# Attention with a position bias and a gated MLP on one core: k and q of the last-row tile change queue, and k gets a second buffer

## The chip, the cores and the metric

The kernel runs on one core of one Trainium2 chip. The metric is the device time of one execution in microseconds (us). The kernel before takes 732.81 us, the median of 3 runs (729.6 to 733.76). One more execution was profiled; it took 731.07 us, with a span of 729.3 us between its first and last instruction. An effect under about 0.5% of the time can't be told from none by such measurements.

## The reference

There are 4 batches, 8 heads, 576 positions and 64 values per head. Each head adds a learned bias, the output of a small network of the distance between two positions, to its scores; after the softmax the result goes through a gated MLP with 512 inputs and 1536 hidden values.

```
scores = scale * np.matmul(q, k.transpose(0, 1, 3, 2))
x = (psi_rel / psi_i)[..., None]
h = np.maximum(x @ w1 + b1, 0.0)
scores = scores + (h @ w2).transpose(2, 0, 1)[None, :, :, :]
attn = softmax(scores)
y = np.matmul(attn, v)                    # back to 2304 x 512
out = ((y @ w_a) * (y @ w_b)) @ w_out
```

## The kernel before

The attention is cut into units. A unit is a batch, a pair of heads and one of two chunks of query rows. The first chunk holds rows 0 to 255, the second rows 256 to 575, so there are 32 units, and the last 16 are of the second chunk. A unit of the first chunk has four tiles of 128 query rows (two per head); a unit of the second chunk has five: A2, B2, A3, B3 and T. T is the mixed last-row tile: it holds the 64 rows that are left (512 to 575) of both heads, 64 partitions for each.

A tile passes through these steps. PE makes the scores into PSUM (`qk`, L533, or L514 for T). DVE adds the bias and takes the row extremum (L561), ACT takes the exponential and the row sum (L566), POOL adds a small number to the sum (L611), DVE takes its reciprocal (L612), POOL scales the row into half precision (`ph`, L596), and DVE makes the low part of it (L599). SP then issues a transposing DMA (L605) that turns `ph` into `pt`. When all tiles of a unit are turned, PE multiplies them with v (`pv`, L657), and ACT and DVE write the result as the input of the MLP (`x`, L670 and L672). The MLP's products (`ab`, L791, and `o`, L835) stand between the attention's products on PE, in an order that the program writes out (`merge`). The attention ends at about 612 us; from there the MLP of the last rows runs alone.

The order on PE is fixed by the program throughout, and that on DVE from the second half of the program. The order on ACT, POOL and SP is chosen by a planner that simulates the program with its own costs: an instruction goes to its engine's list when its inputs and a buffer for its output are there in the simulation, the earlier one of the program first. On the chip every engine and every queue then works through its list in that order, so an instruction that waits holds up all that stand behind it.

SP's queue carries nearly all transfers of this part: the bias rows (`bias`, L498 and L501), k and q of the ordinary tiles (`rk`, `rq`, L423 and L424), v (`rv`, L236), k and q of T (`kt`, L468, two DMAs of 64 partitions, and `qt`, L470), and the transposes (L605). The queue of ACT carries the outputs and, earlier, stores of the bias (L205). The queue of POOL carries DMAs only at the start of the kernel: 16 stores of the bias (also L205).

`load_kt` is called once per unit of the second chunk, at the unit's first tile. `kt` and `qt` live in the pool `xp`, which is opened when the memory of the bias stage (pool `bg2`) comes free. `kt` has one buffer, so the load for the next unit can only start when T's products of this unit have read it; `qt` has two.

Of the kernel before, what the change touches and what calls it, by code (L numbers as in the profile page):

```python
# [9 lines left out]
F32 = mybir.dt.float32  # L10
# [13 lines left out]
HB = S // 2  # L24
# [6 lines left out]
TOK = 256  # L31
# [23 lines left out]
def attention_moe(ctx, tc, q0d, q1d, kd, vd, idn, wp, wa, wb, wo, lsw, lg, rl, out):  # L55
    nc = tc.nc
# [9 lines left out]
    xt, cpool, epool, xpool, ypool = [], [None], [None], [None], [None]  # L66
# [395 lines left out]

    def load_kt(u):
        b, hp, _ = UNITS[u]
        kt = xpool[0].tile([128, 2, HB], F32, tag="kt", name="kt", bufs=1)
        for hf in range(2):
            src = kd[b, hp, :, hf * HB:hf * HB + HB].rearrange("(j d) n -> d j n", j=2)
            nc.sync.dma_start(out=kt[64 * hf:64 * hf + 64], in_=src)  # L468
        qt = xpool[0].tile([128, 2, TAIL], F32, tag="qt", name="qt", bufs=2)
        nc.sync.dma_start(out=qt, in_=q1d[b, hp, :, :, TOK:])  # L470
        st["kt", u], st["qt", u] = kt, qt

    def prep_v(u):
# [209 lines left out]
    def attn_steps():  # L683
        vgen = [None]
        for n in range(NT + 4):
# [16 lines left out]
            for ahead, un in ((a, TILES[n + a][0]) for a in (6, 4, 3, 1, 0, -1) if 0 <= n + a < NT and FIRST[TILES[n + a][0]] == n + a):  # L702
                if un < NP:
                    continue
                if ahead == 6:
                    load_unit(un)
                elif ahead == 4:
                    b, hp, c = UNITS[un]
                    st["raw", un] = *st["raw", un][:2], load_v(b, hp, whole=un < NF)
                elif ahead == 3:  # L710
                    lows[0] = n >= SOON
                    with late():
                        prep_k(un)
                        prep_q(un)
                elif ahead == int(not NF <= un < B * NP):
                    lows[0] = n >= SOON
                    with late():
                        prep_v(un)
                if ahead == 0 and UNITS[un][2]:
                    load_kt(un)  # L720
# [341 lines left out]
```

## Time and profile before

| what | us |
|---|---|
| three runs | 733.76, 729.6, 732.81 |
| profiled execution | 731.07 |
| its span | 729.3 |
| PE busy in the span | 693.7 (95%) |
| DVE busy | 463.0 (63%) |
| ACT busy | 437.4 (60%) |
| POOL busy | 284.0 (39%) |

The profile is that of one execution. Busy time is the time in which an engine had an instruction in work; DMA issues are not counted as busy, except that those of POOL stand in its line. A share over the whole span mixes stages with different limits, and the stage that the change touches, from about 305 to 600 us, has to be read by itself.

### The profile page before, as it was taken

The page shows a single profiled execution, that of the slowest core. Times are in us where ns is not written, and L with a number is a line of the kernel's source. Part 1 is how long each engine was busy: PE and PEld are TensorE (multiplying, and loading weights), DVE is VectorE, ACT ScalarE, POOL GpSimd, SP SyncE. Part 2 cuts the span into 40 slices and gives each one's busy share as a digit, 9 for nine tenths or more (in the row PEclk, how much of TensorE's full clock was granted, in tenths as well). Part 3 has the DMA queues.
Part 4 walks back from the last instruction along what each step waited for, and adds up shares of the span by engine and source line. Part 5 has one row for each costly group of instructions (what it writes and reads, how often), then busy time and mean ns, then how long its engine had stood idle before and what let it go on. Part 6 is the DMA issues. An engine that isn't in the chain of part 4 may idle for free.

```text
span 729.3 us, 15665 instructions
## 1 busy us (share of the span) xinstructions
PE 693.7 (95%) x5535; PEld 534.0 (73%) x5535; DVE 463.0 (63%) x1150; ACT 437.4 (60%) x957; POOL 284.0 (39%) x435
## 2 busy tenths in 40 slices
PE   7889899999999999999899999989999999999997
PEld 1255477778886665777688788878888888888886
DVE  6666388876645676667898889878987871201100
ACT  5887588879967777744566566546655643312310
POOL 3444233336751132333454355435643663311200
PEclk9999999999999999999899999999999999999999
DMA  8989678788745997898999999999999985000001
GB/s 244 329 306 339 231 243 269 225 272 282 257 140 136 213 207 168 205 225 207 243 250 253 252 244 247 252 256 253 245 271 240 224 146 134 1 15 15 2 14 44
DMA packets 178163, 147.69 MB, mean 203 GB/s; under 512 B 125092, under 2 KB 138148, under 8 KB 178084
## 3 DMA queue, kind: packets, MB, share of 16 engines
q1 hardware_dynamic: 170928, 130.91, 71.4%
q10 hardware_dynamic: 5876, 10.93, 5.3%
q0 software_dynamic: 1280, 4.84, 1.8%
q8 instruction: 44, 0.72, 0.4%
q14 instruction: 35, 0.29, 0.1%
HBM read 101.14 MB, written 17.18 MB: 162 GB/s over the span
## 4 chain that ended last, share of the span: by engine, by line
PE 60%; DMA 9%; issue 9%; ACT 7%; DVE 7%; POOL 7%; SPq 1%; POOLq 0%; DVEq 0%; ACTq 0%
PE ab L791 25%; PE o L835 14%; PE pv L657 6%; DMA pt<-ph 5%; PE qk L533 4%; PE psta L184 3%; POOL ph L596 3%; PE tp L629 3%; POOL sm L611 2%; ACT p L566 1%; PE pr L912 1%; DVE ks L438 1%; DVE p L561 1%; POOL gl L811 1%; DVE ph L599 1%
## 5 line engine op out<-in xcount | busy, mean ns | idle before, releaser
L791 PEld LDWEIGHTS <-w16t 128*128 128x128 f16 x2592 | 247.3, 98 | 43.3 <-issue 11.9
L791 PE MATMUL ab<-x,w16t 128*128 128x256 f16 x2304 | 270.2, 273 | 1.0 <-DVE x L672 1.0
L566 ACT ACTIVATE p<-p,mn 128x576 f32<-128x576 f32 x144 | 111.6, 775 | 80.7 <-DVE mn L561 64.2
L599 DVE SCALAR_TENSOR_TENSOR ph<-p,sm,ph 128x64 f16<-128x64 f32 x192 | 106.6, 595 | 29.4 <-POOL ph L596 29.2
L561 DVE CUSTOM_DVE_ANT_0 p<-qk,bias 128x576 f32<-128x576 f32 x143 | 106.6, 747 | 28.4 <-PE qk L533 12.0
L835 PE MATMUL o<-wos,gh 128*128 128x512 f32 x384 | 120.6, 395 | 0.0
L596 POOL TENSOR_SCALAR ph<-p,sm 128x576 f16<-128x576 f32 x96 | 71.8, 748 | 106.7 <-DVE sm L612 96.4
L611 POOL TENSOR_SCALAR sm<-sm 128x1 f32<-128x1 f32 x144 | 54.4, 378 | 146.9 <-ACT p L566 144.6
L811 POOL TENSOR_TENSOR gl<-g,gh 128x256 fp32r<-128x256 f32 x96 | 72.9, 760 | 94.4 <-ACT gh L810 94.1
L775 DVE SCALAR_TENSOR_TENSOR g<-ab,wv,asb 128x256 f32<-128x256 f32 x84 | 40.3, 480 | 77.6 <-ACT asb L799 77.0
L810 ACT CAST gh<-g 128x256 fp32r<-128x256 f32 x96 | 38.8, 404 | 72.8 <-DVE g L775 72.8
L835 PEld LDWEIGHTS o<-wos,gh 128*128 128x128 f32 x384 | 69.5, 188 | 16.9 <-issue 4.5
L835 PE MATMUL o<-wos,gl 128*128 128x512 f32 x192 | 75.0, 391 | 0.0
L533 PE MATMUL qk<-ks,qs 128*128 128x288 f32 x384 | 72.8, 311 | 2.1 <-DVE mn L561 1.2
L533 PEld LDWEIGHTS qk<-ks,qs 128*128 128x128 f32 x384 | 56.1, 189 | 10.9 <-issue 5.3
L617 POOL TENSOR_SCALAR p<-p,sm 128x576 f32<-128x576 f32 x48 | 47.0, 979 | 22.6 <-DVE sm L612 16.1
L799 ACT ACTIVATE asb<-ab,wv 128x256 f32<-128x256 f32 x84 | 39.4, 469 | 25.4 <-PE ab L791 24.8
L657 PE MATMUL pv<-pt,vs 128*64 128x320 f16 (+1 forms) x560 | 42.2, 304 | 7.1 <-DMA pt<-ph 7.1
L657 PEld LDWEIGHTS <-vs 128*64 128x64 f16 x560 | 32.0, 112 | 19.0 <-issue 10.7
L612 DVE RECIPROCAL sm<-sm 128x1 f32<-128x1 f32 x144 | 22.7, 157 | 30.5 <-POOL sm L611 28.7
L835 PEld LDWEIGHTS o<-wos,gl 128*128 128x128 f32 x192 | 36.0, 188 | 7.8
L438 DVE TENSOR_TENSOR ks<-rk,ks 64x576 fp32r<-64x576 f32 x48 | 39.6, 825 | 3.2 <-ACT ks L441 1.8
(105 smaller groups left out, 855.3 us busy)
## 6 DMA issues: line engine op xcount, KB each, us to landing
bias<-bias_d SPq DMA_DIRECT2D x127, 288.0 KB, 4.1
rv<-vd SPq DMA_DIRECT2D x32, 320.0 KB, 4.5
rk<-kd SPq DMA_DIRECT2D x24, 288.0 KB, 3.5
wraw<-wa SPq DMA_DIRECT2D x12, 511.8 KB, 6.2
wraw<-wb SPq DMA_DIRECT2D x12, 511.8 KB, 6.5
wraw<-wo SPq DMA_DIRECT2D x12, 511.8 KB, 5.1
bias_d<-bo ACTq DMA_DIRECT2D x20, 295.5 KB, 3.8
bias_d<-bo POOLq DMA_DIRECT2D x16, 295.5 KB, 6.7
```

The lines of the kernel that those rows point to most:

```text
L438: nc.vector.tensor_tensor(out=ks[ol, j], in0=rk[sl], in1=ks[sl, j].bitcast(F32), op=ALU.subtract)
L533: nc.tensor.matmul(ps[:, hf, :HB], a, b[:, hf * HB:hf * HB + HB], start=(x == 0), stop=(x == len(prods) - 1))
L561: ttr = nc.vector.tensor_tensor_reduce(out=p.rearrange("p (a n) -> p a n", a=2), in0=ps[:, :, :HB], in1=bt.rearrange("p (a n) -> p a n", a=2),
L566: exps.append(nc.scalar.activation(p, p, AF.Exp, bias=mn, scale=-1.0, accum_out=sm))
L596: nc.gpsimd.tensor_scalar(out=ph[:, :S], in0=p, scalar1=rc, scalar2=1.0, op0=ALU.mult, op1=ALU.mult)
L599: ins = nc.vector.scalar_tensor_tensor(out=ph[:, o:o + c1 - c0], in0=p[:, c0:c1], scalar=rc, in1=ph[:, c0:c1], op0=ALU.mult, op1=ALU.subtract,
L611: nc.gpsimd.tensor_scalar(out=sm, in0=sm, scalar1=1e-9, scalar2=1.0 / (PS if u >= NF else 1.0), op0=ALU.add, op1=ALU.mult)
L617: nc.gpsimd.tensor_scalar(out=p, in0=p, scalar1=rc, scalar2=1.0, op0=ALU.mult, op1=ALU.mult)
L657: nc.tensor.matmul(ps[64 * j:64 * j + 64, o:o + N], v[:, j, :], p[:, j * N:j * N + N], start=(x == 0), stop=(x == len(prods) - 1),)
L791: nc.tensor.matmul(ab[:, j], w16[nm, f][:, pw, kk, :], xs[px][:, kk, :], start=(x % (3 * KC) == 0), stop=(x % (3 * KC) == 3 * KC - 1),)
L811: nc.gpsimd.tensor_tensor(out=gl, in0=g, in1=gh.bitcast(F32), op=ALU.subtract)
L835: nc.tensor.matmul(o, g[:, sl], wos[f][:, p], start=(f == 0 and x == 0), stop=(f == FC - 1 and x == 2))
```

## The change

`kt` has two buffers in place of one, and the three DMAs of `load_kt` are issued on POOL's queue in place of SP's. What is loaded, and from where, is the same.

```diff
     def load_kt(u):
         b, hp, _ = UNITS[u]
-        kt = xpool[0].tile([128, 2, HB], F32, tag="kt", name="kt", bufs=1)
+        kt = xpool[0].tile([128, 2, HB], F32, tag="kt", name="kt", bufs=2)
         for hf in range(2):
             src = kd[b, hp, :, hf * HB:hf * HB + HB].rearrange("(j d) n -> d j n", j=2)
-            nc.sync.dma_start(out=kt[64 * hf:64 * hf + 64], in_=src)
+            nc.gpsimd.dma_start(out=kt[64 * hf:64 * hf + 64], in_=src)
         qt = xpool[0].tile([128, 2, TAIL], F32, tag="qt", name="qt", bufs=2)
-        nc.sync.dma_start(out=qt, in_=q1d[b, hp, :, :, TOK:])
+        nc.gpsimd.dma_start(out=qt, in_=q1d[b, hp, :, :, TOK:])
         st["kt", u], st["qt", u] = kt, qt
```

## Rows read from the trace of the kernel before

**Rows 1.** Engines' busy us (instructions), clock, DMA share, GB/s in three stretches.
```profile
330.00:600.00 270.00, 262.22 (x2215) 217.64 (x2208) 225.84 (x535) 157.36 (x362) 130.15 (x203) 0.99 1.11 241
...
350.00:354.00 4.00, 3.87 (x28) 2.90 (x27) 3.91 (x8) 0.63 (x3) 1.13 (x2) 0.50 1.10 293
354.00:358.00 4.00, 4.00 (x32) 3.32 (x31) 3.71 (x10) 3.25 (x8) 2.21 (x4) 0.82 1.07 265
```

**Rows 2.** Waits of PE, 364 to 600 us: total us, times, longest.
```profile
PE pv L657 <- DMA pt<-ph: 3.5, 4, 2.0
```

**Rows 3.** Groups by line and shape, 330 to 600 us: busy us, mean ns, idle before.
```profile
L657 PE MATMUL pv<-pt,vs 128*64 128x320 f16 x420 | 33.2, 312 | 7.1 <-DMA pt<-ph 7.1
```

**Rows 4.** PE in order of time, 322 to 356 us: start, us, what, idle before.
```profile
336.03 0.38 PE L791 MATMUL ab<-x,w16t 128*128 128x256 f16 x2 [0.73 <-DVE x L672]
...
345.83 0.72 PE L514 MATMUL qk<-kt,qt 64*64 64x288 f32 x8
350.13 3.94 PE L657 MATMUL pv<-pt,vs 128*64 128x320 f16 x28 [3.58 <-DMA pt<-ph]
```

**Rows 5.** Chain that ended last: start, us, what.
```profile
344.14 5.95 DMA pt<-ph
...
482.48 6.33 DMA pt<-ph
```

**Rows 6.** SP's queue in order of time, 322 to 356 us.
```profile
326.20 0.33 SPq L501 DMA_DIRECT2D bias<-bias_d  x1
330.49 2.40 SPq L468 DMA_DIRECT2D kt<-kd  x2
...
333.70 2.72 SPq L605 DMA_TRANSPOSE pt<-ph  x2
```

**Rows 7.** Waits of SP's queue, 305 to 364 us.
```profile
SPq L468 <- PE qk L514: 3.9, 1, 3.9
...
SPq L468 <- DMA bias_d<-bo: 1.2, 1, 1.2
```

**Rows 8.** SP's queue in order of time, 455 to 600 us.
```profile
477.38 0.66 SPq L468 DMA_DIRECT2D kt<-kd  x1
478.14 1.77 SPq L605 DMA_TRANSPOSE pt<-ph  x1
479.96 0.61 SPq L468 DMA_DIRECT2D kt<-kd  x1
480.63 0.60 SPq L470 DMA_DIRECT2D qt<-q1d  x1
...
482.48 1.96 SPq L605 DMA_TRANSPOSE pt<-ph  x1
...
583.11 1.31 SPq L605 DMA_TRANSPOSE pt<-ph  x1
```

**Rows 9.** DVE in order of time, line L599, around 338, 477 and 582 us.
```profile
337.97 0.95 DVE L599 SCALAR_TENSOR_TENSOR ph<-p,sm,ph 128x64 f16<-128x64 f32 x2 [1.26 <-POOL ph L596]
...
477.40 0.94 DVE L599 SCALAR_TENSOR_TENSOR ph<-p,sm,ph 128x64 f16<-128x64 f32 x2
...
582.10 0.95 DVE L599 SCALAR_TENSOR_TENSOR ph<-p,sm,ph 128x64 f16<-128x64 f32 x2 [2.36 <-POOL ph L596]
```

**Rows 10.** T's products, by tile: ns min/median/max, first and last start us.
```profile
L514 PE MATMUL qk<-kt,qt x128: 402/428/453, 329.7 to 594.6; 64*64 64x288 f32 x128
```

**Rows 11.** Line L205 over the whole span: POOL's DMA issues, ns min/median/max.
```profile
L205 POOL DMA_DIRECT2D bias_d<-bo x16: 530/533/3730, 9.8 to 34.1; - x16
```

**Rows 12.** Groups of DVE by line, 9 to 35 us: busy us, mean ns.
```profile
L174 DVE TENSOR_SCALAR w16t<-u,lgs 128x528 f32<-128x528 f32 (+13 forms) x43 | 16.2, 443 | 3.5 <-PE psta L184 3.4
```

**Rows 13.** Waits of DVE, 330 to 600 us: total us, times, longest.
```profile
DVE ph L599 <- POOL ph L596: 22.2, 64, 3.0
DVE p L561 <- DMA bias<-bias_d: 6.6, 4, 2.9
```

## The prediction, made before the changed kernel was run

> **What bounds the kernel now.** I read the busy time by stretches first, then the waits of PE, then the chain that ended last, then PE and SP's queue in order of time, and last what POOL and DVE have to spare.
>
> In the stretch that the change touches PE is busy for 262.22 of 270 us [rows 1]. So the most that any change of the attention's supply can win here is the idle 7.8 us and what a lowered clock cost. The waits name one cause: of the idle time before PE's main product with v, 7.1 us are put down to the transposes `pt<-ph` [rows 3], and 3.5 us of it, in four waits, lie behind 364 us [rows 2]. The largest single wait is ahead of that: PE ends T's products at 346.55 and starts `pv` at 350.13, 3.58 us later [rows 4]. What it waits for is a transpose that SP issued at 344.14 and that landed 5.95 us later [rows 5].
>
> Why was it issued so late? DVE had finished that tile at 338.92 (337.97 and 0.95) [rows 9]; transposes and DVE's pairs both come in the program's order, so the n-th belongs to the n-th, and this one waited 5.22 us for its turn. SP's queue shows the reason: it issues a bias load that ends at 326.53 and then nothing until the second `kt` at 330.49 [rows 6]. Its wait is 3.9 us on T's own products, L514 [rows 7]: with one buffer the load for the next unit has to wait until PE has read this one, and every transpose stands behind it, the next at 333.70 [rows 6]. The later part has the same illness without a long wait. Around 477 us SP goes from one issue to the next with 0.05 to 0.1 us between them [rows 8]; a tile that DVE ended at 478.34 (477.40 and 0.94) [rows 9] is transposed at 482.48 [rows 8], 4.14 us late, lands 6.33 us after that at 488.81 [rows 5], and there the 2.0 us wait of [rows 2] falls. Where SP's list is thin, the delay is gone: DVE ends at 583.05 (582.10 and 0.95) [rows 9], SP transposes at 583.11 [rows 8]. So SP's issue is a server that is nearly full, and the last transpose of a unit is what PE sees of it.
>
> **The change part by part.**
>
> *The second buffer of k* takes the wait of 3.9 us away. The transposes queued behind it start up to 4 us earlier, and *the three issues that leave SP* add to this: 0.66, 0.61 and 0.60 us, 1.87 us for a unit [rows 8], while T's products come every 17.66 us (594.6 less 329.7, over 15) [rows 10]. That is 10.6% of SP's time. The transpose that held PE at 350.13 would be issued at about 339 to 340 in place of 344.14, and even with 5.95 us to land it is there by 346, when PE asks for it at 346.55. I remove the 3.58 us in full.
>
> PE's clock is then not lost either. After that idle time the granted clock was 0.50 of full speed, the lower of its two levels, in 350 to 354 us, and 0.82 in the next 4 us [rows 1]: 4 x 0.50 + 4 x 0.18 = 2.72 us of full speed. I remove this too, since PE has no other pause near it as long as this one.
>
> The four later waits (3.5 us) [rows 2] and the 0.73 us that PE waited at 336.03 for `x` [rows 4] come from transposes and DVE work that are late by less than the 2 to 4 us that a thinner list gives back. Of these 4.2 us I take 3.0, between 0 and 4.2, since what comes late next is unknown. The bias loads, for which DVE waited 6.6 us [rows 13], are issued earlier as well; PE doesn't see that directly, and I put nothing for it.
>
> *The three issues that POOL gets* are 48 in all. One of POOL's own issues takes 0.53 us, 3.73 at most (the longest of 16) [rows 11]. At 0.53 that is 25.4 us on an engine that is busy for 130.15 of 270 us [rows 1]. Behind an issue stand `sm` (L611) and `ph` (L596) of the next tile, and behind these DVE, which is busy for 225.84 us [rows 1] and has 44.2 us to spare, 22.2 of them spent waiting for POOL already [rows 13]. So even if every issue hit its line in full, 25.4 us fit into the 44.2. PE would see it only where a tile is late by more than the lead that SP gives back. I take 1.0 us, near the lower end of 0 to 25.4, because DVE's spare time covers it; if that cover were gone, the first rival below holds. A gain below zero I exclude: POOL gets nothing back.
>
> *The start* costs something. The first `kt` waited 1.2 us for the last store of the bias stage, whose memory it takes [rows 7]. On SP only transfers stood behind that wait; on POOL the softmax of a running tile does. Both first units' loads, six issues, may now come at once. Bounds: 0 (all of it in POOL's idle time) and 1.2 + 3.73 + 5 x 0.53 = 7.6 us (all in a row, the first as slow as POOL's first issue). I take 1.5, near the lower end: just then PE has the output products `o` to do, which need no attention.
>
> *What could be late for T itself*: the loads can be asked for a unit ahead, as `qt` with its two buffers was; a unit is 17.66 us, and I put nothing for it. The bytes are the same.
>
> Sum on the profiled execution: 731.07 - 3.58 - 2.72 - 3.0 + 1.0 + 1.5 = 724.3 us. That execution lies 1.7 us under the median of the three runs (732.81). The four executions together have a mean of 731.8, and from this the same 6.8 us give 725.0 us, my forecast; its own range is 720 to 729.
>
> **The rivals.**
>
> *POOL's issue becomes DVE's bound* (slower). Place: the list of POOL, in front of `sm` and `ph`. The price is that of one issue, and it decides from 44.2 / 48 = 0.92 us on, where POOL's issues use up DVE's spare time. With the middle of the two ends by ratio, 1.41 us, 48 issues take 67.7 us, 23.5 over the spare time; less the 6.3 us of the first stall, the time is 731.8 + 23.5 - 6.3 = 749 us; with 3.73 us, some 860. For it: in this stretch DVE is busy for 84% of the time [rows 1], and none of POOL's issues was measured there. Against it: the median of 16 issues is 0.53 us [rows 11], and DVE ran 43 operations, 16.2 us, in those same 26 us [rows 12]. The Trainium skill, "SBUF — State Buffer", section "SBUF: two separate sides", speaks for this rival: it says that the descriptors of a DMA from GpSimd's queue can't be written while DVE holds the port that the two share, and gives 620 ns grown to about 3100 for one such DMA (section on the bandwidth pool); by that, an estimate from the page, 48 issues would cost 119 us more. The trace doesn't bear it out where it can be seen: 0.53 us beside a busy DVE [rows 11, 12]. Chance 0.12.
>
> *The transposes are limited by the DMA engines, not by SP's issue.* The mean busy share is 1.11 of the engines [rows 1], and the transpose at 482.48 took 6.33 us to land with its issue taking 1.96 [rows 5, 8]. Then an earlier issue lands no earlier, except after SP's standstill at 326.5. Only the stall at 346.5 and its clock go: 731.8 - 6.3 + 2.5 = 728.0 us. Against it: at 344.14 and 482.48 the waiting before the issue, 5.2 and 4.1 us, was as long as the landing. Chance 0.15.
>
> *Nothing that can be measured changes.* SP's place as the last to be late is taken by DVE (busy for 84% of the stretch) or by POOL at the start, so that `pv` waits as before: a start near its upper bound (7.6 us) alone uses up what is won, 731.8 - 9.3 + 7.6 + 1.0 = 731.1 us. Or the planner puts the loads late into POOL's list, and the transposes gain while T waits. The Trainium skill, "DMA: Bandwidth & Descriptors", section "Issuing engines are not separate DMA queues", leans this way: all queues end on the same engines, and another issuer saves only issue time, usually small beside the transfer. Here issue time is what is scarce: 0.05 to 0.1 us between SP's issues [rows 8]. Chance 0.13.
>
> **How the numbers follow.** The forecast has 0.60, the rivals 0.12, 0.15 and 0.13. An effect under 0.5% (3.7 us) is about what a measurement can't tell from none. The forecast lies in "faster" but for the 0.03 of its upper end; the DMA rival at 728.0 is split, 0.10 to 0.05; of the last rival 0.10 is "same", 0.01 slower and 0.02 faster. Faster 0.69, same 0.18, slower 0.13. The range is 718.5 to 734: it holds the forecast with the gain of all waits and no cost, the DMA rival and most of the last, and leaves out the slow rival and a small rest above and below.
>
> **What would show it.** Right: in the waits of SP no `kt` behind L514; transposes in 326 to 347 us within about 1 us of DVE's end, and elsewhere less late than 2 to 4 us; no pause of PE before the first `pv` of 128x320, and a granted clock of 1.00 after it; issues of POOL near 0.53 us. Wrong: issues of POOL over 0.92 us or DVE's waits for `ph` well over 22.2 us (the slow rival); transposes issued early that land late (the DMA rival); new waits of PE between 306 and 330 us (the start was sized too low). A gain over 10 us would mean that PE's list had pauses that the profile doesn't show.

## The result, and the profile after

The changed kernel takes 737.58 us (median of 12 runs, 734.85 to 742.2), the kernel before beside it 729.74 us (12 runs, 726.0 to 735.98). The ratio is 1.0092 with a 95% interval of 1.0066 to 1.0117: slower by some 6.7 us by the ratio (the medians lie 7.8 us apart), where 725.0 us were forecast, and outside the forecast's range. The profiled execution took 738.23 us, with a span of 736.5 us. In the program, PE's and DVE's lists stand as before; those of POOL, SP and ACT are planned anew.

I read the waits of PE first (view of waits, the changed kernel, PE, 305 to 600 us: who waited for whom, total us, times, longest).

```profile
PE qk L533 <- DVE ks L438: 6.5, 2, 3.7
PE pv L657 <- DMA pt<-ph: 3.1, 1, 3.1
PE qk L533 <- DVE qs L457: 1.2, 2, 0.6
```

The waits for transposes fell to 3.1 us from the 7.1 of [rows 3]. A new line stands above them: PE waits twice for `ks`, the low part of k of an ordinary tile, for which [rows 2 to 4] have no counterpart. The places, in PE's order of time (changed kernel; start, us, what, idle before):

```profile
318.19 0.82 PE L533 MATMUL qk<-ks,qs 128*128 128x288 f32 x2 [2.75 <-DVE ks L438]
...
343.14 0.82 PE L533 MATMUL qk<-ks,qs 128*128 128x288 f32 x2 [3.72 <-DVE ks L438]
...
358.43 2.09 PE L657 MATMUL pv<-pt,vs 128*64 128x320 f16 x28
...
427.27 3.70 PE L657 MATMUL pv<-pt,vs 128*64 128x320 f16 x28 [3.13 <-DMA pt<-ph]
```

The pause ahead of the first `pv` of 128x320 [rows 4] is gone: that product starts at 358.43 with no idle time before it (8.3 us later than in the kernel before, so the transposes had that much more time). Two pauses stand ahead of it instead, and one of 3.13 us behind it. The stretches around them (changed kernel; length, busy us of PE, weight loads, DVE, ACT and POOL, granted clock, DMA share, GB/s):

```profile
310.00:318.00 8.00, 5.44 (x27) 4.28 (x26) 3.02 (x7) 2.80 (x6) 6.12 (x10) 1.00 1.00 191
318.00:324.00 6.00, 5.21 (x33) 3.83 (x34) 5.00 (x13) 2.11 (x5) 1.86 (x4) 0.50 0.88 210
...
342.00:348.00 6.00, 4.27 (x17) 3.13 (x18) 5.48 (x15) 2.51 (x5) 1.91 (x4) 0.50 1.04 254
...
427.00:430.00 3.00, 2.73 (x22) 2.37 (x23) 2.53 (x7) 0.77 (x2) 2.76 (x5) 0.53 1.14 269
440.00:600.00 160.00, 160.00 (x1360) 133.35 (x1359) 137.97 (x328) 96.54 (x223) 94.67 (x149) 1.00 1.11 242
```

Each of the three pauses is followed by a granted clock of about half, the lower of the two levels; before, from 305 to 600 us, only the one pause of [rows 4] was, with the 0.50 of [rows 1]. From 440 to 600 us PE is busy without a gap at full clock, which the kernel before was not (it waited 2.0 us there [rows 2]). So the change does what it promised late, and loses more early. In 310 to 318 us POOL is the busiest engine, with 6.12 of 8 us. Its order of time shows with what (changed kernel, POOL):

```profile
310.60 1.26 POOL L468 DMA_DIRECT2D kt<-kd  x2 [3.52 <-ACT ks L441]
311.84 0.73 POOL L470 DMA_DIRECT2D qt<-q1d  x1
...
314.55 0.19 POOL L611 TENSOR_SCALAR sm<-sm 128x1 f32<-128x1 f32 x1
...
336.51 1.25 POOL L468 DMA_DIRECT2D kt<-kd  x2 [3.57 <-PE qk L514]
337.74 0.72 POOL L470 DMA_DIRECT2D qt<-q1d  x1
338.51 0.74 POOL L596 TENSOR_SCALAR ph<-p,sm 128x576 f16<-128x576 f32 x1
```

These are two holds, and I call them A and B.

- **Hold A, 307 to 314.5 us.** The first `kt` stands still for 3.52 us at the head of POOL's list, then six issues follow in a row, and only then `sm` of a tile whose exponential ACT ended at 309.29. The row names ACT's `ks`; the store of the bias for which SP waited before [rows 7] was issued at 306.59 and lands at about the same time, and the profile doesn't part the two.
- **Hold B, 333 to 338.5 us.** With two buffers the load that has to wait is the third unit's, which takes the first unit's buffer. It waits 3.57 us for T's first products (L514), the same wait as SP's 3.9 us before [rows 7], and now `ph` of two tiles stands behind it.

DVE passes both on (changed kernel, DVE):

```profile
314.77 0.17 DVE L612 RECIPROCAL sm<-sm 128x1 f32<-128x1 f32 x1 [2.71 <-POOL sm L611]
...
339.29 0.95 DVE L599 SCALAR_TENSOR_TENSOR ph<-p,sm,ph 128x64 f16<-128x64 f32 x2 [7.59 <-POOL ph L596]
...
342.24 1.54 DVE L438 TENSOR_TENSOR ks<-rk,ks 64x576 fp32r<-64x576 f32 x2
```

The `ks` that PE needs is behind these in DVE's list, so a DMA that waits on POOL reaches PE by way of `sm`, `ph` and `ks`. PE has no lead at the place that hold A hits: in the kernel before it already waited 0.91 us there, for `qs`, which stands right behind `ks` in DVE's list (kernel before, PE in order of time):

```profile
316.24 0.53 PE L533 MATMUL qk<-ks,qs 128*128 128x288 f32 x2 [0.91 <-DVE qs L457]
```

Last, the sizes. By line, over the whole span (ns min/median/max, first and last start us):

```profile
L468 POOL DMA_DIRECT2D kt<-kd x32: 598/616/649, 310.6 to 566.9; - x32
L470 POOL DMA_DIRECT2D qt<-q1d x16: 717/721/731, 311.8 to 567.5; - x16
L514 PE MATMUL qk<-kt,qt x128: 402/428/453, 335.5 to 601.8; 64*64 64x288 f32 x128
```

DVE's waits, 330 to 600 us:

```profile
DVE ph L599 <- POOL ph L596: 31.2, 62, 7.6
DVE p L561 <- DMA bias<-bias_d: 1.1, 1, 1.1
```

The transposes' time from issue to landing, by line, 364 to 600 us:

```profile
DMA to landing us min/median/max: 3.2/5.1/9.2
```

T's first products start 5.8 us later than before and the last ones 7.2 us [rows 10]; 0.5 us of this stands already at 305 us. So in this execution most is lost between 305 and 335 us, where hold A is.

### The profile page after: what moved, and what is told of

It is laid out like the page before. It is cut to its first block, busy times and chain, and to the rows that moved or that the text cites. A ratio compares the mean times of both kernels' runs of the same rounds, so it can differ in the third digit from the quotient of the medians.

```text
span 736.5 us, 15617 instructions
## 1 busy us (share of the span) xinstructions
PE 698.2 (95%) x5535; PEld 536.4 (73%) x5535; DVE 463.4 (63%) x1150; ACT 437.7 (59%) x957; POOL 311.7 (42%) x483
## 4 chain that ended last, share of the span: by engine, by line
PE 44%; POOL 3%; DVE 3%; issue 2%; DMA 1%; ACT 1%; DVEq 0%; POOLq 0%; ACTq 0%
PE ab L791 22%; PE o L835 14%; PE pv L657 4%; PE qk L533 3%; POOL ph L596 2%; DVE ph L599 1%; DMA pt<-ph 1%; PE qk L514 1%; POOL gl L811 0%; POOL sm L611 0%; POOL kt L468 0%; DVE sm L612 0%; DVE g L775 0%; ACT p L566 0%; DVE xt L672 0%
## 5 line engine op out<-in xcount | busy, mean ns | idle before, releaser
L599 DVE SCALAR_TENSOR_TENSOR ph<-p,sm,ph 128x64 f16<-128x64 f32 x192 | 106.4, 594 | 38.2 <-POOL ph L596 37.7
L611 POOL TENSOR_SCALAR sm<-sm 128x1 f32<-128x1 f32 x144 | 51.3, 356 | 137.4 <-ACT p L566 134.5
L533 PE MATMUL qk<-ks,qs 128*128 128x288 f32 x384 | 74.9, 317 | 9.0 <-DVE ks L438 6.5
```

The source lines that it names most:

```text
L533: nc.tensor.matmul(ps[:, hf, :HB], a, b[:, hf * HB:hf * HB + HB], start=(x == 0), stop=(x == len(prods) - 1))
L599: ins = nc.vector.scalar_tensor_tensor(out=ph[:, o:o + c1 - c0], in0=p[:, c0:c1], scalar=rc, in1=ph[:, c0:c1], op0=ALU.mult, op1=ALU.subtract,
L611: nc.gpsimd.tensor_scalar(out=sm, in0=sm, scalar1=1e-9, scalar2=1.0 / (PS if u >= NF else 1.0), op0=ALU.add, op1=ALU.mult)
```

## The experiments

Each ratio is against runs of the kernel before on the same chip, with its 95% interval. In kernels with an added line the line numbers stand one to nine higher.

### The two halves of the change

**Only the second buffer** (the kernel before with `bufs=2` for `kt`, on SP).

```
-        kt = xpool[0].tile([128, 2, HB], F32, tag="kt", name="kt", bufs=1)
+        kt = xpool[0].tile([128, 2, HB], F32, tag="kt", name="kt", bufs=2)
```

> One part alone: two buffers for k, all loads still on SP. Theory (the loss comes from POOL's list): nothing of it is here, SP's wait of 3.9 us for T's first products goes, and with it the stall of 3.6 us and the lowered clock behind it, up to 7.7 us less than the kernel before: 722 to 728 us. SP stays as full as it was, so the later waits of 3.5 us stay. Rival (the second buffer itself does harm, by the memory it takes or by how the planner orders the rest): 735 to 740 us.

Measured: 730.58 us, 0.9979 (0.9946 to 1.0012); neither forecast holds. Two rows say why (this kernel, SP's waits from 305 to 364 us and PE's from 305 to 600):

```profile
SPq L468 <- PE qk L514: 3.0, 1, 3.0
PE pv L657 <- DMA pt<-ph: 5.5, 4, 3.1
```

The wait on SP didn't go with the second buffer. It passed to the third unit's load, which the planner lists ahead of T's first products; a pause of 3.1 us ahead of `pv` stays.

**Only the queue** (the changed kernel with `bufs=1`).

> The other part alone: the loads on POOL's queue, k with one buffer. Theory: POOL's list now waits for T's products of the unit before at every load, the first of them again at 330 to 337 us, and the start has four issues in a row in place of six: 735 to 745 us. Rival (the second buffer lets the loads be pulled ahead, and only that does harm): with one buffer there is less to pull ahead, 725 to 732 us.

Measured: 733.49 us, 1.0038 (1.0011 to 1.0065), between the two. Its PE row has both new pauses (waits of PE, 305 to 600 us), so the holds come with the queue, not with the buffer. With one buffer four issues follow the first wait in place of six, and the first pause is 1.5 us in place of 2.75:

```profile
PE qk L533 <- DVE ks L438: 5.3, 2, 3.7
```

**Later loads** (the changed kernel, each load asked for only after the latest `ph` of POOL).

```
-                    load_kt(un)
+                    with tc.issue_after(phs[-1].ins):
+                        load_kt(un)
```

> The changed kernel, with the loads of k and q for T put behind POOL's latest ph in its list, so that they can't be pulled ahead of the softmax of running tiles. Theory (POOL's list is held up twice: at the start by six loads that wait for the bias stage's last store, later by the third unit's load that waits for T's first products): both holds go. They cost PE 2.4 us of idle time and 3.5 us of clock in 305 to 330 us, and 4.3 and 3.4 us in 330 to 364 us, 13.6 us in all; so the time is 736.5 - 13.6 = 723 us, 719 to 728, faster than the kernel before by 0.3 to 1.5%. Rival (an issue on POOL is itself too dear for the softmax, 48 times 2 us for three): the number of issues is the same, so the time stays at 735 to 740 us.

Measured: 738.36 us, 1.0078 (1.0043 to 1.0114): the forecast of my theory missed. Neither pause ahead of `ks` is left, but the edit brought losses of its own (waits of PE, 305 to 600 us): six waits for transposes, and T waited for its own `qt`:

```profile
PE pv L658 <- DMA pt<-ph: 6.8, 6, 2.0
...
PE qk L515 <- DMA qt<-q1d: 1.7, 2, 1.0
```

So it tells nothing against the holds.

**Without the loads** (the changed kernel; the loads of `kt` and `qt` are left out for the last 14 units, which use the second unit's).

```
-                    load_kt(un)
+                    if un < B * NP + 2:
+                        load_kt(un)
+                        kept = st["kt", un], st["qt", un]
+                    else:
+                        st["kt", un], st["qt", un] = kept
```

> The changed kernel, which leaves out the loads of k and q for T of the last 14 units (they use those of the first two). The start's six issues stay as they are, the load that waits for T's first products is gone, and neither SP nor POOL issues any later. Theory: the start's 5.9 us (2.4 idle, 3.5 clock) stays lost, the second hold's 7.7 us goes, perhaps the later stall of 3.1 us at 424 as well: 724 to 729 us. Rival (42 issues on POOL at 2 us for three are what costs): all of the loss but the start's goes and SP is free too, under 722 us.

Measured: 730.41 us, 0.9997 (0.9972 to 1.0022). This lies above the range of my theory, and farther from the rival's. Hold B and 42 issues are gone and it is still no faster than before: hold A is there (a pause of 2.8 us ahead of `ks`), and so is one of 2.8 us at the first `pv` of 128x320. This one stands although no load of `kt` is left on SP; what SP does wait for is the last first-chunk `pv`. (PE's waits from 305 to 600 us, SP's from 305 to 364, then SP and PE in order of time.)

```profile
PE qk L533 <- DVE ks L438: 2.8, 1, 2.8
```
```profile
SPq L605 <- PE pv L657: 5.7, 1, 5.7
```
```profile
333.99 0.72 PE L514 MATMUL qk<-kt,qt 64*64 64x288 f32 x8
336.43 2.75 SPq L605 DMA_TRANSPOSE pt<-ph  x2
...
353.60 3.43 PE L657 MATMUL pv<-pt,vs 128*64 128x320 f16 x28 [2.80 <-DMA pt<-ph]
```

### The two holds, one at a time

In the changed kernel some units' loads go back to SP; the rest stays on POOL.

```
+        q = nc.sync if u < B * NP + 3 else nc.gpsimd      # first three units on SP
+        q = nc.sync if u == B * NP + 2 else nc.gpsimd     # or: the third alone
+        q = nc.sync if u < B * NP + 2 else nc.gpsimd      # or: the first two
...
-            nc.gpsimd.dma_start(out=kt[64 * hf:64 * hf + 64], in_=src)
+            q.dma_start(out=kt[64 * hf:64 * hf + 64], in_=src)
```

> The changed kernel, but the loads of the first three second-chunk units (nine DMAs) are requested on SP again; the other 39 stay on GpSimd. Theory (the change loses its time in two holds of GpSimd, at its first load, which waits for the bias stage's last store, and at the third unit's load, which waits for the first T products): both holds go, and with them the PE pauses of 2.75 and 3.72 us and the half clock behind each; the pause ahead of the first 128x320 pv returns. 729 to 733 us where the kernel before takes 730 to 731. Rival (the 39 later issues on GpSimd and the transposes that land late beside them carry the loss): 735 to 740.

> The changed kernel with the third unit's load alone back on SP: the hold of GpSimd at that load goes, the one at its first load stays. Theory (each hold costs its PE pause and the half clock behind it): the pause near 318 us stays at 2.5 to 3 us, the one near 343 us goes, and the time comes out between the changed kernel and the one with three units on SP: 731 to 736 us. Rival (the first hold alone, or the second alone, carries the loss): 736 to 740, or 727 to 730.

> The changed kernel with the loads of the first two second-chunk units back on SP, the third and all later ones on GpSimd: the hold at the first load goes, the one at the third unit's load stays. Theory (each hold costs by itself; the first some 0.9% and the second 0.3%, from the run with the third alone on SP and that with all three): 0.998 to 1.002 of the kernel before, with a pause of PE of 3 us or more near 340 us. Rival (the second hold costs as much as the first once it stands alone): 1.004 to 1.008.

| hold A | hold B | kernel | us | ratio (95%) |
|---|---|---|---|---|
| no | no | three units on SP | 729.53 | 0.9964 (0.9933 to 0.9995) |
| no | yes | first two on SP | 732.38 | 1.0011 (0.9989 to 1.0033) |
| yes | no | third on SP | 736.21 | 1.0058 (1.0030 to 1.0085) |
| yes | yes | the changed kernel | 737.58 | 1.0092 (1.0066 to 1.0117) |

Waits of PE from 305 to 600 us, of the first, the second and the third of these:

```profile
PE pv L658 <- DMA pt<-ph: 5.2, 2, 2.8
```
```profile
PE qk L534 <- DVE ks L438: 3.7, 1, 3.7
```
```profile
PE qk L534 <- DVE ks L438: 2.7, 1, 2.7
```

The pause near 318 us comes and goes with A, the one at 335 to 343 us with B, and the times add up within the noise: A costs 0.0081 to 0.0094 (5.9 to 6.9 us of 731), B 0.0034 to 0.0047 (2.5 to 3.4 us). By the intervals of the table, each of these differences is uncertain by some 0.004 either way, the mean of B's two by some 0.003; so A is clear, and B is smaller and just clear of none. The planner orders its lists anew for each kernel, so the four differ in more than the two holds; that it is these that count rests on the pauses coming and going with them. In the cells without B the third unit's load still waits for T's first products, but on SP:

```profile
SPq L469 <- PE qk L515: 3.0, 1, 3.0
```

That is three units on SP; with the third alone it is 4.0 us. So B is the price of having this wait on POOL in place of SP. With neither hold, the same 39 loads on POOL are no loss. The expectations held but for 0.2 us in the run with the third on SP, whose 736.21 us also lies at the edge of its rival's range (one hold carries the loss). Between 318 and 324 us the granted clock is 1.00 with neither hold, where the changed kernel has 0.50:

```profile
318.00:324.00 6.00, 6.00 (x50) 4.97 (x50) 4.71 (x13) 3.31 (x7) 2.19 (x4) 1.00 0.92 217
```

### What the first stall was worth

With the holds gone the kernel still has 2.8 us ahead of the first `pv`. A second wait could be the cause: the first second-chunk transposes wait for the last first-chunk `pv`, because their `pt` lies over memory which that `pv` reads. In the changed kernel SP stands 5.7 us in it (its waits, 305 to 364 us):

```profile
SPq L605 <- PE pv L657: 5.7, 1, 5.7
```

Four kernels with all loads on SP came first: the second chunk's memory laid out anew (`pt`, `xt`, `ph`, `pt`, so that the first unit's `pt` lies elsewhere), the loads asked for after the latest transpose, both, and both with another order of the memory (`ph`, `xt`, `pt`, `pt`) and loads after the fifth-latest transpose.

```
+        trs.append(nc.sync.dma_start_transpose(out=st["pt", u][:, :, o:o + 128], in_=ph))
...
+                    with tc.issue_after(trs[-1].ins):     # or trs[-5]
+                        load_kt(un)
...
+            pre["ph"] = cpool[0].tile([128, 2 * S], F16, tag="ph", name="ph", bufs=2)
             xt.extend(cpool[0].tile([128, KC, B * TAIL], F16, name=f"xt{p}") for p in range(2))
+            pre["pt", B * NP + 1] = cpool[0].tile([128, 9, 640], F16, tag="pt1", name="pt", bufs=1)
+            pre["pt", B * NP] = cpool[0].tile([128, 9, 640], F16, tag="pt0", name="pt", bufs=1)
```

> The kernel before with the memory layout alone: the first second-chunk unit's pt doesn't lie over the first chunk's, kt keeps one buffer on SP. Theory (two waits in a row): SP still waits for the first T products before the second unit's kt, ahead of that transpose, so nothing changes: 729 to 732 us. Rival (the wait for pv was the only one that counted): 724 to 727.

> The kernel before with two buffers for kt and each load requested on SP only after the latest transpose issued by then; the layout is as before. Theory (two waits in a row): SP's wait for kt is gone, but the first second-chunk transpose still waits for the last first-chunk pv, so the pause ahead of the first 128x320 pv stays at 2 to 3.6 us: 728.5 to 732 us. Rival (the prediction's reason: the wait for kt was the only one): 724 to 727.

> The kernel before, all on SP, with two changes: kt has two buffers and each load is requested only after the latest transpose issued by then, and the second chunk's memory is laid out so that the first second-chunk unit's pt doesn't lie over that of the last first-chunk units. Theory (two waits in a row held the first second-chunk transposes: SP for kt, then the transpose itself for the last first-chunk pv): with both gone, the 3.58 us ahead of the first 128x320 pv go, and the half clock behind it: 724 to 727 us where before takes 730 to 731. Rival (something else is late next at that place, as GpSimd's ph or the transposes' landing): 729 to 732.

> The kernel before, all loads on SP, with the memory order ph, xt, pt, pt, two buffers for kt, and each load requested after the fifth-latest transpose. Theory (two waits in a row): the pause ahead of the first 128x320 pv goes without GpSimd's help: 724 to 728 us where before takes 730 to 733. Rival (SP is too full, so that its transposes stay 2 to 4 us late and the pause stays or moves): 729 to 734.

Measured: layout alone 732.62 us, 1.0004 (0.9975 to 1.0032), as expected but not for that reason: in the new layout `ph` lies over the same memory, so POOL took the wait, and PE paused 3.2 us ahead of `ks`. Later loads alone 741.49, 1.0123 (1.0075 to 1.0171); both 741.94, 1.0156 (1.0107 to 1.0205): they were too late, and T waited for `qt` 11.4 us in the one and 6.6 in the other, so they settle nothing on the layout. The fourth 735.91, 1.0037 (1.0000 to 1.0075): slower than either forecast, nearer the rival, though its first `pv` of 128x320 starts at 347.31 us without a pause, as my theory had it. One row each of layout alone (POOL's waits, 305 to 364 us), later loads alone and the fourth (PE's, 305 to 600):

```profile
POOL ph L603 <- PE pv L664: 5.0, 1, 5.0
```
```profile
PE qk L515 <- DMA qt<-q1d: 11.4, 5, 3.6
```
```profile
PE pv L665 <- DMA pt<-ph: 7.5, 6, 3.6
```

The clean pair has the first three units on SP, the rest on POOL, and the third unit's load alone asked for after the fifth-latest transpose, so that no load waits for T's first products on either queue (`with tc.issue_after(trs[-5].ins) if un == B * NP + 2`); one of the two also has the layout of the fourth.

> The same without the memory order: SP's wait for kt is gone, the first second-chunk transpose still waits for the last first-chunk pv. Theory (two waits): the pause ahead of the first 128x320 pv stays at 2 to 3.6 us, 727 to 731 us where before takes 730 to 733. Rival (the wait for kt is the only one that counts): pause under 1 us, 723 to 727.

> As the run with the first three units' loads on SP, and with two more edits: the third unit's load is requested only after the fifth-latest transpose, so SP doesn't stand in its wait for the first T products, and the second chunk's memory is ordered ph, xt, pt, pt, so that the first second-chunk unit's pt lies over nothing that the last first-chunk pv reads (its second unit's pt does, and that is written some 15 us later). Theory (two waits in a row held the first second-chunk transposes): both are gone, the 2.8 to 3.6 us ahead of the first 128x320 pv go, with the half clock behind them: 723 to 727 us where before takes 730 to 733. Rival (DVE's and GpSimd's part of that tile is late next, or the transposes' landing): 727.5 to 731.

Measured: without the layout 728.27 us, 0.9961 (0.9937 to 0.9985); with it 727.35 us, 0.9950 (0.9926 to 0.9974), the fastest of all kernels, 3.6 us below the kernel before beside it (730.95). The first time lies in the range of my theory (two waits), its pause of 0.17 us in that of the rival; the second lies between the two ranges. SP and PE in order of time, without the layout, then with it:

```profile
330.21 0.72 PE L516 MATMUL qk<-kt,qt 64*64 64x288 f32 x8
332.66 2.74 SPq L607 DMA_TRANSPOSE pt<-ph  x2
...
348.04 2.09 PE L659 MATMUL pv<-pt,vs 128*64 128x320 f16 x28 [0.17 <-DMA pt<-ph]
367.54 2.09 PE L659 MATMUL pv<-pt,vs 128*64 128x320 f16 x28 [3.03 <-DMA pt<-ph]
```
```profile
327.64 3.96 SPq L614 DMA_TRANSPOSE pt<-ph  x2
329.61 0.72 PE L516 MATMUL qk<-kt,qt 64*64 64x288 f32 x8
...
347.26 2.09 PE L666 MATMUL pv<-pt,vs 128*64 128x320 f16 x28
363.88 2.09 PE L666 MATMUL pv<-pt,vs 128*64 128x320 f16 x28 [0.43 <-DMA pt<-ph]
```

SP's waits without the layout, 305 to 364 us, and the clock around its second pause (length, busy us of the engines, granted clock, DMA share, GB/s):

```profile
SPq L607 <- PE pv L659: 4.5, 1, 4.5
```
```profile
367.50:371.00 3.50, 3.46 (x42) 3.06 (x42) 2.83 (x7) 1.70 (x5) 3.33 (x6) 1.00 1.18 273
```

There are two waits in a row, and both delay the transposes. Counted from the start of T's first products, SP issues the next pair of transposes 4.0 us later in the kernel before (333.70 [rows 6], 329.7 [rows 10]), 2.45 us later without the wait for `kt`, and 1.97 us earlier with the layout too. So the wait for `kt` was worth 1.5 us of that delay (0.7 against the kernel with three units on SP, where it is 3.15), and the wait for `pv`, which stands right behind it, another 4.4.

The first pause falls to 0.17 us without the layout, from 3.58 [rows 4] and from the 2.8 with three units on SP, which is one edit away. So taking away the wait for `kt` removed it here, as predicted. But that wait isn't the whole cause: the kernel without the 14 loads has no `kt` on SP, the same delay (2.44 us, 336.43 against 333.99), and a pause of 2.80. What tells these two kernels apart wasn't tried. With both waits gone there is no such pause, in the fourth of the four kernels and with the layout here. My theory of two waits was right about the delay and wrong about the pause that it forecast. And none of it shows in the time beyond the noise: 0.9964 with the pause (three units on SP), 0.9961 without it, 0.9950 with the layout. Without the layout a pause of 3.03 us stands one unit later, against 0.43 with it; that the second wait makes it is likely but not shown.

A long pause isn't always followed by the lower clock. Behind this one of 3.03 us the granted clock is 1.00, and the 28 products take 2.09 us where they took 3.94 in [rows 4].

### What the rest of the queue change gives

**All on SP, no load in a wait for T's first products** (the kernel before with two buffers; the third and all later loads after the fifth-latest transpose).

> The kernel before with two buffers for kt, all loads on SP, those of the third and later units requested only after the fifth-latest transpose: as the run with three units on SP and the third paced, but with the other 39 loads on SP too. Theory (GpSimd's queue does give something, since SP is nearly full): slower than that run, 0.998 to 1.003 of before, with pauses ahead of pv behind 364 us of 2 us or more. Rival (all of the gain is that no load stands in a wait, whichever queue it is on): 0.994 to 0.997.

Measured: 736.56 us, 1.0077 (1.0050 to 1.0104), slower than the ranges of both theory and rival, and far from the 0.9961 of its twin with 39 loads on POOL. But SP without that order takes 0.9979 (only the second buffer, above), so this difference isn't the price of the 39 issues alone. One of its pauses is another list held up by a DMA (ACT's waits from 560 us, PE's from 305):

```profile
ACT gx L827 <- DMA gx<-g_d: 7.8, 1, 7.8
PE ab L793 <- DVE g L777: 3.1, 1, 3.1
```

How much the queue gives by itself stays open: one pair of kernels shows nothing measurable (0.9964 against 0.9979), the other 1.2%, of which that pause and the clock behind it are a part.

## Why the prediction was wrong

The forecast was 6.8 us less, the measurement is 6.7 us more. Of these 13.5 us the start makes some 5, a wait that was not in the sum some 3, and a gain that didn't come some 5 to 6.

**The step that failed, and turned the sign, is "The start".** I sized it at 1.5 us, "near the lower end" of 0 to 7.6, because PE has other products to do just then. It measured 5.9 to 6.9 us (hold A). The bound was built from the right parts (a wait of the first load, six issues in a row), and POOL was held for nearly all of it: 3.52 us, then six issues to 314.5, 7.4 us together. What I missed is the way on: `sm` and `ph` on POOL, then `ks` on DVE, then PE, which has no lead there (the 0.91 us before), and then the half clock behind PE's pause. Products that need no attention stand there, as I wrote, but PE's list has `qk` among them. The sign that I had set for this came, a new wait of PE between 306 and 330 us.

**Hold B was not in the sum.** I wrote that the second buffer "takes the wait of 3.9 us away", and of the early loads "I put nothing for it". Here the second buffer moves the wait one unit on; the planner lists that unit's load as early as its own times allow, ahead of T's first products, and the wait of [rows 7] stood again on POOL, 3.57 us long, in front of two tiles' `ph`. Cost: 2.5 to 3.4 us. I named what stands behind an issue on POOL, but for all loads after the start I priced only issues, never a wait.

**The gain was too large.** The three terms are 9.3 us, 8.3 less the 1.0 for issues. With neither hold and 39 of the 48 loads on POOL the kernel gains 2.6 us (0.9964), and the clean pair 2.9 and 3.7.

*The first stall (-3.58) and its clock (-2.72)* had a cause that was right in part: the wait for `kt` holds the transposes, but not by "up to 4 us" of delay, only by 1.5, because SP waits for the last first-chunk `pv` right behind it. In the changed kernel the pause is gone, but PE comes there 8.3 us later.

The clock isn't won, it falls after the new pauses instead. As an estimate: in the means over the runs, span times (1 minus the granted clock) is 3.9 us for the kernel before (35 runs beside the first four experiments) and 9.6 us for the changed one (12 runs), and the time less that is 727.8 and 728.1. So by this estimate nearly all that was lost is clock, behind pauses that cost about as much in themselves as those removed. In the clean pair it is 3.6 and 3.7 us, 3.5 for the kernel before beside them: on the mean no clock is won there either.

*The later waits (-3.0 of 4.2)* came out near nothing: behind 364 us PE waits 3.1 us against 3.5 [rows 2], in one place in place of four; from 440 us on it waits no more. DVE's waits for the bias fell as said, 6.6 us [rows 13] to 1.1, for which the sum had nothing.

**Issues on POOL (+1.0).** They took 0.62 and 0.72 us, not 0.53, under the 0.92 from which the slow rival was to decide; what they cost PE wasn't measured apart. DVE waited 31.2 us for `ph` against 22.2 [rows 13], most of the rise in the one wait of 7.59. The slow rival had the sign right and the mechanism wrong: it is not the price of an issue on a full engine but two waits at the wrong place. The rival that nothing measurable changes named a start near its upper bound, and so came nearest to what happened; it kept the whole gain and left out B. The rival that the DMA engines limit the transposes wasn't tried by a run of its own; what bears on it stands below.

The sum with terms measured in other kernels: 0.9964 for what is left of the gain, +0.0094 for A alone and +0.0047 for B alone make 1.0105; measured 1.0092 (1.0066 to 1.0117).

## What to carry to other kernels

A DMA moved from a queue to a compute engine brings its waits along, and whatever follows in that engine's list now waits too: ask of every moved load what its first and its buffer-reusing requests wait for, and who stands behind them. A further buffer may not remove such a wait but pass it on to a later load, which a planner may put in the very same place, as here; keep the first loads on the queue where only transfers wait, or tie the reusing load to something that comes later. Where a pause of PE is followed by the lower clock, price it with that, but don't count on winning it back (a pause elsewhere can lose it again), and price a bound by the lead that PE has at that place. Before a wait is taken off the sum, ask what the same queue waits for right behind it.

## What the hardware showed that was not expected

**The latest transposes land later in kernels with loads on POOL's queue.** From 364 to 600 us the longest landing is 9.2 us in the changed kernel, 9.3 with three units on SP, 9.3 and 8.6 in the clean pair; it is 6.9 in the kernel before, 6.8 with the second buffer alone, 7.1 without the 14 loads and 7.0 with all on SP. The other kernels fit: 8.0 to 10.9 with loads on POOL there, 6.1 to 7.6 without. The medians overlap (4.7 to 6.1 against 4.2 to 5.0). Each is one execution. The pauses near 420 us (3.13 us in the changed kernel) fit to that; that they come from it was not tried.

**No issue on POOL was long.** Of 32 issues of `kt` in the changed kernel the longest took 0.649 us and the median 0.616, in a stretch in which DVE is busy most of the time (137.97 of 160 us from 440 to 600). The Trainium skill, "SBUF — State Buffer", section "SBUF: two separate sides" (its part on the bandwidth pool), gives some 620 ns for a DMA of this queue that runs alone, and about 3100 for one overlapped with a DVE copy that holds the shared port. The issues lie near the first figure, though the row is that of the issue and not of the whole DMA, and nothing near the second is seen here; whether DVE held that port in this stretch, no run shows.
